# Moving the G products to another PSUM pool and filling TensorE's early waits with unused products

## Chip, cores, metric

One core of one Trainium2 chip. The metric is device microseconds (us) of one execution. A kernel's executions spread by about ±0.15 to 0.2% here, so each comparison uses several runs of both kernels on the same chip.

## The reference

```python
def _attn_ref(x):                      # x: (8, 3008, 256)
    X = np.fft.fft(x, axis=1)
    X = np.fft.fft(X, axis=2)
    return X.real.astype(np.float32)

def _moe_ref(x, w_in, w_out):          # 24064 tokens, 256 -> 2048 -> 256
    h = x @ w_in
    r = np.maximum(h, 0.0)
    g = r * r
    return (g @ w_out).astype(np.float32)
```

## The kernel before

The second transform is folded into `w_in`: for each of eight column pairs j, `G` is a product of `w_in` with cosine and sine tables, and `gE` a product with a column of alternating signs. The weights arrive as 64-bit floats and are converted on VectorE and ScalarE. The first batch's sequence transform ("groups", tiles `pd`) runs first (0 to 60 us); then eight *conversion steps* each convert one pair of weights, make its G, and do one step of the main loop; from about 127 us the main loop alone keeps TensorE full.

Three pools of PSUM matter. `psh` (tag "h", two banks) holds the `ph` products of the front. `psd` (tag "d", two banks) holds the transform's products, `pe`, and later the output transposes. `psm` (four banks) holds the accumulators mA to mD.

```python
psh = ctx.enter_context(tc.tile_pool(name="psh", bufs=2, space=PSUM))
psd = ctx.enter_context(tc.tile_pool(name="psd", bufs=2, space=PSUM))
psm = ctx.enter_context(tc.tile_pool(name="psm", bufs=1, space=PSUM))
# ... cut ...
def load_win(j):
    w = ep.tile([P, 2, CH], F32, name="win", tag="sB" if j % 2 else "sA")
    finish = convert(w, pair_in(j))
    def products():
        for tab, G, n in ((cosd, G1, P), (sind, G2, P - 1)):
            ps = psh.tile([P, CH], F32, name="pg", tag="h")
            for i in range(2):
                nc.tensor.matmul(ps[0:n], tab[:, i], w[:, i], start=i == 0, stop=i == 1)
            nc.scalar.copy(G.rearrange(...)[j], ps[0:n].rearrange(...))
        ps = psd.tile([P, CH], F32, name="pe", tag="d")
        # ... four products of one column into ps[:, 0:2] ...
        nc.scalar.copy(gE[:, j::NJ], ps[:, 0:2])
    return finish, products
# ... cut: one step of the main loop, i < NJ being the conversion steps ...
g = front(b, k0, n, j, between)        # TensorE ph, VectorE he, g, g (twice)
if i < NJ:
    s = combine(n, g)                  # ScalarE Relu, Square; then POOL
for f in products:
    f()                                # G and gE of the next pair
products = [next_weight() for _ in range(2 if i + 2 < NJ else 1 if i < NJ else 0)]
```

## Time and profile before

| | before |
|---|---|
| median of its runs in this comparison | 2052.55 us (2048.85 to 2054.36, 6 runs) |
| span of the profiled run | 2051.2 us |
| TensorE busy | 98% |
| first front on VectorE | at 60.12 us |
| main loop alone on TensorE | from about 127 us |

On TensorE's timeline of the kernel before, one conversion step at full clock:

```profile
93.88 1.13 PE L228 MATMUL pg<-win,sind 128*127 128x256 f32 x4
94.85 0.95 PE L234 MATMUL pe<-altd,win 128*128 128x1 f32 x8
95.66 1.09 PE L450 MATMUL mA<-g,wout 128*128 128x251 f32 x4
```

pe follows the sine product at once, and the products of an earlier step follow pe. Keep the order pg, pe, mA to mD, then the next front: TensorE takes its products in this order, so whatever pe waits for, the next front waits for as well.

### The profile page before, as it was taken

Reading aid. Unit: us, or ns where it says so; the run is one execution under the profiler, and the core shown is the slowest. Engines: PE = TensorE matmul, PEld = TensorE weight load, DVE = VectorE, ACT = ScalarE, POOL = GpSimd, SP = SyncE. Lnnn points to the kernel's source line nnn. Section 1 sums busy time; section 2 is a strip of 40 time slices with the busy share of each in tenths; the row PEclk is TensorE's granted clock in tenths of the full one; section 3 lists DMA queues with packets and bytes.
Section 4 is the critical chain, followed back from the end, with each engine's and each line's share of the span. In section 5 each row is a group of like instructions: output and inputs, shape, how many; then the busy total and the mean of one; then the engine's idle time right before and its main releaser. Section 6 shows DMA issues by size and latency. Waiting matters only on the chain.

```text
span 2051.2 us, 27084 instructions
## 1 busy us (share of the span) xinstructions
PE 2009.5 (98%) x9464; PEld 1744.3 (85%) x9464; DVE 1337.1 (65%) x3275; ACT 950.3 (46%) x1067; POOL 1206.1 (59%) x1763
## 2 busy tenths in 40 slices
PE   6799999999999999999999999999999999999998
PEld 3578888888888888888888888888888888888887
DVE  6888665776567755777557775577656776555554
ACT  1554444444444544455444544454444444445443
POOL 0466655665566655666556665566655675556654
PEclk9799999999999999999999999999999999999999
DMA  6223000110011000011001100011001100000000
GB/s 178 87 58 59 29 11 31 40 37 21 11 39 43 26 26 30 26 31 47 11 26 36 38 29 11 31 41 36 21 11 41 41 11 16 31 11 11 21 11 20
DMA packets 66104, 68.45 MB, mean 33 GB/s; under 512 B 26297, under 2 KB 56969, under 8 KB 65968
## 3 DMA queue, kind: packets, MB, share of 16 engines
q1 hardware_dynamic: 64892, 66.21, 11.3%
q8 instruction: 74, 1.21, 0.2%
q10 hardware_dynamic: 1076, 0.52, 0.1%
q14 instruction: 62, 0.51, 0.1%
HBM read 42.03 MB, written 24.68 MB: 33 GB/s over the span
## 4 chain that ended last, share of the span: by engine, by line
PE 94%; DVE 4%; DMA 1%; issue 0%; ACT 0%; SPq 0%; DVEq 0%; ACTq 0%
PE mA L450 16%; PE mC L450 16%; PE mB L450 16%; PE ph L407 16%; PE ph L408 16%; PE mD L450 8%; PE pd L344 5%; PE po L492 2%; DMA xt<-in_x_dram 1%; PE pg L228 1%; DVE he L410 0%; DVE fd L211 0%; DVE fs L213 0%; DVE g L412 0%; DVE g L413 0%; DMA raw<-in_moe_w_in_dram 0%
## 5 line engine op out<-in xcount | busy, mean ns | idle before, releaser
L421 ACT ACTIVATE g<-g 128x1004 f32<-128x1004 f32 (+1 forms) x384 | 399.4, 1040 | 759.3 <-DVE g L413 487.4
L410 DVE SCALAR_TENSOR_TENSOR he<-Et,gE,ph 128x251 f32<-128x251 f32 (+1 forms) x768 | 362.1, 471 | 580.6 <-PE ph L408 580.0
L427 POOL TENSOR_TENSOR s<-g 128x251 f32<-128x251 f32 (+1 forms) x384 | 251.7, 655 | 744.1 <-ACT g L422 719.9
L407 PE MATMUL ph<-Pt,G 128*128 128x251 f32 (+1 forms) x1536 | 453.1, 376 | 1.2 <-DVE g L413 0.6
L408 PE MATMUL ph<-Qt,G 127*128 127x251 f32 (+1 forms) x1536 | 452.2, 375 | 0.2 <-DVE Qt L357 0.2
L422 ACT ACTIVATE g<-g 128x1004 f32<-128x1004 f32 (+1 forms) x384 | 399.3, 1040 | 12.1
L450 PE MATMUL mA<-g,wout 128*128 128x251 f32 (+1 forms) x1536 | 391.9, 377 | 0.0
L450 PE MATMUL mC<-s,wsum 128*128 128x251 f32 (+1 forms) x1536 | 389.8, 375 | 0.0
L412 DVE TENSOR_TENSOR g<-he,ph 128x251 f32<-128x251 f32 (+1 forms) x768 | 320.4, 417 | 58.9 <-DVE he L410 0.5
L407 PEld LDWEIGHTS ph<-Pt,G 128*128 128x128 f32 x1536 | 288.9, 189 | 43.6 <-issue 3.7
L408 PEld LDWEIGHTS ph<-Qt,G 127*128 127x128 f32 x1536 | 291.7, 190 | 36.6 <-DVE Qt L357 0.6
L450 PEld LDWEIGHTS mC<-s,wsum 128*128 128x128 f32 x1536 | 292.1, 190 | 35.6
L413 DVE TENSOR_TENSOR g<-he,ph 128x251 f32<-128x251 f32 (+1 forms) x768 | 314.2, 409 | 0.0
L450 PEld LDWEIGHTS mA<-g,wout 128*128 128x128 f32 x1536 | 282.2, 190 | 37.3 <-issue 4.0
L428 POOL TENSOR_TENSOR s<-s,g 128x251 f32<-128x251 f32 (+1 forms) x384 | 288.6, 752 | 30.1
L429 POOL TENSOR_TENSOR s<-g 128x251 f32<-128x251 f32 (+1 forms) x384 | 290.4, 756 | 0.0
L430 POOL TENSOR_TENSOR s<-g,s 128x251 f32<-128x251 f32 (+1 forms) x384 | 262.1, 683 | 0.0
L450 PE MATMUL mB<-g,wsum 128*128 128x251 f32 (+1 forms) x768 | 226.0, 375 | 0.0
L450 PE MATMUL mB<-s,wout 128*128 128x251 f32 (+1 forms) x768 | 225.5, 375 | 0.0
L450 PE MATMUL mD<-s,wout 128*128 128x251 f32 (+1 forms) x768 | 225.0, 374 | 0.0
L450 PEld LDWEIGHTS mB<-g,wsum 128*128 128x128 f32 x768 | 146.2, 190 | 17.9
L450 PEld LDWEIGHTS mB<-s,wout 128*128 128x128 f32 x768 | 145.1, 189 | 18.0
(77 smaller groups left out, 1331.6 us busy)
## 6 DMA issues: line engine op xcount, KB each, us to landing
xt<-in_x_dram SPq DMA_DIRECT2D x24, 512.0 KB
out_dram<-os SPq DMA_DIRECT2D x94, 125.0 KB
out_dram<-os SPq DMA_DIRECT2D x80, 126.0 KB
xt<-in_x_dram SPq DMA_DIRECT2D x16, 384.0 KB
Et<-e_dram SPq DMA_DIRECT2D x7, 752.5 KB
raw<-in_moe_w_in_dram SPq DMA_DIRECT2D x16, 256.0 KB
raw<-in_moe_w_out_dram SPq DMA_DIRECT2D x16, 256.0 KB
xt<-in_x_dram SPq DMA_DIRECT2D x8, 480.0 KB
```

Source lines behind the costliest of these rows:

```text
L407: nc.tensor.matmul(hP, G1[:, fs], pt[:, ks], start=True, stop=True)
L408: nc.tensor.matmul(hQ, G2[:, fs], qt[:, ks], start=True, stop=True)
L410: nc.vector.scalar_tensor_tensor(out=t, in0=et[:, ks], scalar=gE[:, fc:fc + 1], in1=hP, op0=ALU.mult, op1=ALU.add)
L412: tt(out=g[:, h, 0, 0:n], in0=t, in1=hQ, op=ALU.add)
L413: tt(out=g[:, h, 1, 0:n][:, ::-1], in0=t, in1=hQ, op=ALU.subtract)
L421: act(v, v, AF.Relu)
L422: act(v, v, AF.Square)
L427: gt(out=s1, in0=g21, in1=g22, op=ALU.add)
L428: gt(out=s2, in0=s1, in1=g11, op=ALU.subtract)
L429: gt(out=s3, in0=g11, in1=g21, op=ALU.subtract)
L430: gt(out=s4, in0=g12, in1=s2, op=ALU.subtract)
L450: nc.tensor.matmul(acc[nm][:, i, 0:n], w, v[:, 0:n], start=j == 0 and i == 0, stop=j == NJ - 1, skip_group_check=True)
```

## The change

Its intent: G's products shall not wait for the banks of the front ("h"), and TensorE's clock shall not fall to half while it waits in the transform. G's products move to pool "d"; 116 products of the identity with itself, whose result nothing reads, go to an unused column range of mD's bank.

```diff
+    acc = {"mD": psm.tile([P, 2, CH], F32, name="mD", tag="mD")}
+    awoken = 0
+    def awake(n):
+        nonlocal awoken
+        for _ in range(n):
+            nc.tensor.matmul(acc["mD"][:, 1, 0:P], ident, ident, start=not awoken, stop=True, skip_group_check=True)
+            awoken += 1
@@ load_win
-                ps = psh.tile([P, CH], F32, name="pg", tag="h")
+                ps = psd.tile([P, CH], F32, name="pg", tag="d")
@@ groups_at
             groups[i]()
+            if i % 5 in (0, 3):
+                awake(6)
@@ start
     start()
+    awake(32)
     for_p(0)
     finish, products = begun
     finish()
     products()
+    awake(12)
```

(The accumulators of the first block reuse the mD already made.)

More of the change, by code (lines that the diff above doesn't have):

```diff
@@ L431, in combine @@
         return s
-    acc = {}
     def back(n, j, g, s, final):
         if j == 0:
-            for nm in ("mA", "mB", "mC", "mD"):
+            for nm in ("mA", "mB", "mC") if len(acc) == 1 else ("mA", "mB", "mC", "mD"):
                 acc[nm] = psm.tile([P, 2, CH], F32, name=nm, tag=nm)
```

## The prediction

> **What bounds the kernel now.** I read the page from the top. The engine table, then the slices of the span, then the costliest groups:
>
> ```profile
> PE 2009.5 (98%) x9464; PEld 1744.3 (85%) x9464; DVE 1337.1 (65%) x3275; ACT 950.3 (46%) x1067; POOL 1206.1 (59%) x1763
> ...
> PE   6799999999999999999999999999999999999998
> PEclk9799999999999999999999999999999999999999
> ...
> L407 PE MATMUL ph<-Pt,G 128*128 128x251 f32 (+1 forms) x1536 | 453.1, 376 | 1.2 <-DVE g L413 0.6
> ```
>
> TensorE is the bound from about 127 us to the end (one step is 4.67 us of products back to back; 384 steps). The change touches only instructions ahead of that. Each slice is 51 us, so only slices 1 to 3 can move: the transform of the first batch (0 to 60 us) and the eight steps in which the weights are converted (60 to 127 us). The second slice has the lowest clock, 0.7.
>
> I then read the stretches of 10 us and the timeline of each engine there. In the conversion steps VectorE is the bound: one step runs from its first "he" at 101.03 to the next at 110.69, 9.66 us with hardly a hole, while TensorE has 7.8 us of work in it at full clock (L228 and L234 3.0, L450 3.1, L407/L408 1.7). The holes of VectorE, from its timeline:
>
> ```profile
> 77.29 0.81 DVE L211 SCALAR_TENSOR_TENSOR fd<-raw,fd 128x512 uint32<-128x512 uint32 x1 [0.91 <-ACT fd L204]
> 91.42 0.47 DVE L410 SCALAR_TENSOR_TENSOR he<-Et,gE,ph 128x251 f32<-128x251 f32 x1 [1.59 <-PE ph L408]
> 122.44 0.47 DVE L410 SCALAR_TENSOR_TENSOR he<-Et,gE,ph 128x251 f32<-128x251 f32 x1 [1.60 <-PE ph L408]
> ```
>
> Three holes of the first kind (0.91, 0.66, 0.95) and two of the second, both where TensorE ran at half clock. What the change aims at is on TensorE's timeline:
>
> ```profile
> 81.04 1.13 PE L228 MATMUL pg<-win,cosd 128*128 128x256 f32 x4 [1.80 <-DVE g L413]
> 82.20 1.74 PE L228 MATMUL pg<-win,sind 128*127 128x256 f32 x4
> 83.72 1.71 PE L234 MATMUL pe<-altd,win 128*128 128x1 f32 x8
> ```
>
> G's product waits for "g L413" (the front before it must give back its bank of the pool "h"), although its operand win was ready at 79.82; 1.2 us later than it could be.
>
> The third reading is ScalarE's order in the same steps, which decides the case:
>
> ```profile
> 93.86 1.04 ACT L421 ACTIVATE g<-g 128x1004 f32<-128x1004 f32 x1 [4.36 <-DVE g L413]
> 94.94 1.04 ACT L422 ACTIVATE g<-g 128x1004 f32<-128x1004 f32 x1
> 95.88 0.63 ACT L229 COPY G<-pg 128x256 f32<-128x256 f32 x2
> 96.40 0.17 ACT L236 COPY gE<-pe 128x2 f32<-128x2 f32 x1
> 96.45 0.74 ACT L203 ACTIVATE fd<-fd,ramp 128x512 f32<-128x512 uint32 x1
> ```
>
> G's copy stands behind the two activations of the front, so it starts 2.05 us after the front's last g (93.83), whenever pg was ready.
>
> **What the Trainium skill says.** "TensorE: Matmul & The Clock Gate", Part 1 (The HAM clock gate): the clock is halved after an idle window of some 3.4 us and restored after a busy one; the window runs free. The trace agrees: the granted clock falls to 0.50 at 72.3 and 82.6 us and comes back at 79.1 and 89.4, that is after two windows of 3.4. But it also falls after windows that were not idle (the gap at 81.04 is 1.80 us)[...]. The same page, in its table of the array, calls ScalarE a strict FIFO: the rows above agree, G's copy never passes L421. "PSUM — Partial Sum Buffer", The four PSUM rules, gives one bank to a product; the pools h and d have two buffers each, and the other four banks hold mA to mD, so nothing can be had for pg without sharing.
>
> **The change part by part.**
>
> (a) pg moves to pool "d". The order of instructions is unchanged; I listed the waits of the changed program. pg now waits for win, no longer for g: start up to 1.2 us earlier. But cos, sin and pe are now three tiles of one step in two buffers: pe takes the buffer of the cos product and must wait for G's copy. The list indeed shows a ScalarE wait on the first pe of each step, which the kernel before has not. In the step of 93.83: pe started 94.85; now the first copy ends at 95.88+0.31=96.19, and pe starts near 96.3, 1.45 us later. That has three costs.
> 1. gE's copy (96.40) slips to about 97.2, and L203, L204 behind it by 0.8; L211 of VectorE waits as at 77.29. What such a hole really costs is read from whole steps: 69.75 to 79.74 (with it) is 9.99, 101.03 to 110.69 (without) 9.66, so 0.35; conversions beside POOL's work run slower and a late one escapes that. Six steps have it in place of three: **+1.1 us**.
> 2. TensorE: pe 0.8, products of a step 3.0, first pair of the next front 0.85 and 0.15 to come out: 96.3+4.8=101.1 against VectorE's need at 101.0 to 101.4. At full clock that just fits. But between the end of pg (about 94.0 when started at win) and the end of pe lie 3 us and more in which TensorE does nothing, or one-column products. I expect the half clock in four of the five steps with an L450 group ahead of the front. A spell of 6.8 us with some 6 us of work in it costs up to 3 us of work; as part falls into gaps I take 2.1 on average, less 0.4 of slack, 1.7. 4x1.7=6.8, less the 3.2 that the kernel before loses so: **+3.6 us**.
> 3. In the last converting step TensorE becomes the bound. There pe started 125.94, with g at 124.92; it would now start at 124.92+2.5=127.4, all after it later by **+1.4 us**.
>
> (b) Unused products. 32 ahead of all, 12 behind the first pe, 6 behind each of the 12 transform groups: 116. One is two passes of 128 columns. Passes of 94 columns follow each other at 0.11 us at full clock (first 0.43 us of the group at 38.68), 256 columns at 0.21; I take 0.11 to 0.12 for 128: 6 products are 1.35 us, 12 are 2.7. The first 32 take from 7 us (full clock) to 14 us (half) and fit ahead of 13.13, when win arrives.
> What a warm clock can gain in the transform is at its end:
>
> ```profile
> 54.66 4.10 PE L344 MATMUL pd<-sinT,wQ 128*127 128x376 f32 x6 [0.80 <-DVE dc L359]
> ...
> 58.79 0.55 DVE L357 TENSOR_TENSOR Qt<-dc,pd 127x376 f32<-127x376 f32 x1 [3.37 <-PE pd L344]
> ```
>
> Six passes at half clock, 4.1 us; at full clock 2.05. VectorE waits 3.37 of it, so 2 us come back there, and 0.6 to 0.9 earlier, where the "da" copies come sooner. Against it: 1.35 us of unused products stand between the last group and the first front in TensorE's order; L407 (58.54, before Qt was ready) can no longer start ahead of that. Following the groups through with 1.35 behind each, the first front comes 1.9 us earlier if the clock is high throughout, and 0.3 us later if the wait for the table (cosT landed at 22.05; unused products end near 18.3) halves it again so that groups and fillers crawl until about 28. I hold the second for likelier: **-0.5 us**.
>
> Sum: +1.1+3.6+1.4-0.5 = +5.6; 2051.9+5.6 = **2057.5 us**. Accumulators mD: same engine, in order, nothing.
>
> **The rivals.**
> - pg's earlier start is worth what it looks like: the holes at 91.42 and 122.44 go and the phase stays warm, -4 to -7 us (2046). For it: PE would have 7.8 of 10 us. Against it: pe sits behind pg in TensorE's order, and what comes behind pe sets the front.
> - The new wait is there but the clock holds: +1.1+1.4-0.5, 2054. For it: a gap of 1.80 at 102.39 did not trip the clock. Against: the new gap is nearly twice that.
> - Every step cold, two windows each: +10 to +12, 2063.
> - Nothing visible: the runs of before spread over 2050.55 to 2054.36 already, perhaps by where the free window falls.
>
> **Range and chances.** Rivals two and three set most of the range, 2050.5 to 2064. Two per cent is 41 us; all that the change can reach is about 127 us, and VectorE's conversions alone fill most of it. So within 2%: 0.985; slower 0.01; faster 0.005.
>
> **What would show it.** In the profile after: a ScalarE wait (copy of G) ahead of pe in each step of 60 to 135 us; pg's wait on g gone, on win instead; six holes on L204 of 0.7 to 1; clock at 0.5 in most of those steps and fronts waited for by VectorE; the handover to back-to-back products (before about 124 us) at 128 to 134 us. At 20 to 60 us a higher clock than 0.57 to 0.75, first "he" between 58.2 and 60.5. I am wrong if pe does not wait, if the clock stays high in spite of the gaps, or if the transform gains more than 2 us.

## More of the kernel before

The two stretches that the change can reach, of the kernel before; the columns are stretch, its length, then busy us (and instructions) of PE, PEld, DVE, ACT and POOL, then granted TensorE clock, DMA share, GB/s:

```profile
0.00:60.00 60.00, 39.09 (x105) 23.73 (x106) 39.97 (x113) 9.43 (x19) 0.70 (x6) 0.89 0.59 161
60.00:135.00 75.00, 63.23 (x260) 51.02 (x259) 64.24 (x116) 45.28 (x76) 40.73 (x56) 0.86 0.27 81
```

No engine is full in either: these are chains of waits between TensorE, VectorE and ScalarE, with a clock below full.

## The result

| | median | range | runs |
|---|---|---|---|
| before | 2052.55 us | 2048.85 to 2054.36 | 6 |
| changed | 2059.69 us | 2058.63 to 2065.06 | 6 |

Ratio 1.0042, 95% interval 1.0028 to 1.0056: slower by about 8.6 us (0.0042 of 2052), well inside 2%. A ratio is the mean time of one kernel's fast runs over that of the other's of the same rounds, so not quite the ratio of the medians.

The same two stretches of the changed kernel:

```profile
0.00:60.00 60.00, 54.67 (x338) 45.96 (x339) 40.30 (x114) 9.45 (x19) 0.70 (x6) 0.97 0.58 162
60.00:135.00 75.00, 56.55 (x233) 45.93 (x232) 58.48 (x107) 44.25 (x74) 39.37 (x54) 0.84 0.27 81
```

The clock in the transform rose from 0.89 to 0.97, as intended. Yet in the second stretch TensorE and VectorE did less work in the same 75 us: 233 records of products instead of 260 (each product of 32-bit floats shows as two records, "x2"; the recorded texts call one a pass). Its cause, first on TensorE's timeline of the changed kernel (L239 and L245 are the former L228 and L234, L459 the former L450):

```profile
92.92 1.03 PE L239 MATMUL pg<-win,sind 128*127 128x256 f32 x4
96.29 1.46 PE L245 MATMUL pe<-altd,win 128*128 128x1 f32 x8 [2.34 <-ACT G L240]
97.61 2.02 PE L459 MATMUL mA<-g,wout 128*128 128x251 f32 x4
```

pg starts without waiting for g now, but pe waits 2.34 us for ScalarE's copy of G. The products behind it take 2.02 us in place of 1.09. The clock by the microsecond (the number before the last two) shows why:

```profile
95.00:96.00 1.00, 0.00 (x0) 0.00 (x0) 0.96 (x3) 1.00 (x2) 0.00 (x0) 1.00 0.00 0
96.00:97.00 1.00, 0.71 (x6) 0.71 (x6) 0.97 (x2) 0.51 (x2) 0.87 (x2) 0.88 0.39 31
97.00:98.00 1.00, 1.00 (x5) 1.00 (x6) 1.00 (x2) 0.21 (x2) 1.00 (x2) 0.50 0.80 297
```

ScalarE's timeline of the same step:

```profile
95.88 0.63 ACT L240 COPY G<-pg 128x256 f32<-128x256 f32 x2
97.79 0.16 ACT L247 COPY gE<-pe 128x2 f32<-128x2 f32 x1 [1.28 <-PE pe L245]
97.84 0.72 ACT L203 ACTIVATE fd<-fd,ramp 128x512 f32<-128x512 uint32 x1
```

G's copy starts at the very moment it started before (95.88), because it stands behind the front's activations; pg's earlier product gained nothing. gE's copy came 1.39 us later than the 96.40 of before, and L203 with it. VectorE then waits twice in this step, once for each of them:

```profile
99.36 0.83 DVE L211 SCALAR_TENSOR_TENSOR fd<-raw,fd 128x512 uint32<-128x512 uint32 x1 [1.30 <-ACT fd L204]
...
104.65 0.47 DVE L421 SCALAR_TENSOR_TENSOR he<-Et,gE,ph 128x251 f32<-128x251 f32 x1 [2.74 <-PE ph L419]
```

**A ledger.** Everything ahead of the main loop lies on one chain, so the span can be cut at four moments read from the timelines: the table's landing (start of the first 128x189 product), VectorE's first "he", the first "he" of the seventh front (six conversion steps later), and the start of the last pe, behind which TensorE runs without a stop.

| us | table landed | transform | six steps | to the last pe | rest | span |
|---|---|---|---|---|---|---|
| before | 22.08 | 38.04 | 62.32 | 3.50 | 1925.3 | 2051.2 |
| changed | 20.38 | 39.47 | 66.60 | 4.99 | 1925.4 | 2056.8 |
| difference | -1.70 | +1.43 | +4.28 | +1.49 | +0.1 | +5.6 |

The landing is before any of the changed work and differs from run to run. The transform, at a higher clock, became longer. Five waits of VectorE in the changed kernel's trace show where:

```profile
26.21 0.25 DVE L368 TENSOR_TENSOR db<-da,pd 128x94 f32<-128x94 f32 x1 [1.59 <-ACT da L363]
...
33.10 0.55 DVE L368 TENSOR_TENSOR Pt<-dc,pd 128x376 f32<-128x376 f32 x1 [1.53 <-PE pd L355]
...
52.34 0.69 DVE L211 SCALAR_TENSOR_TENSOR fd<-raw,fd 128x512 uint32<-128x512 uint32 x1 [2.43 <-ACT fd L204]
...
57.66 0.55 DVE L368 TENSOR_TENSOR Qt<-dc,pd 127x376 f32<-127x376 f32 x1 [1.41 <-PE pd L355]
...
59.85 0.47 DVE L421 SCALAR_TENSOR_TENSOR he<-Et,gE,ph 128x251 f32<-128x251 f32 x1 [1.18 <-PE ph L419]
```

The wait for Qt, which the warm clock was to shorten, did: 3.37 to 1.41. But L211 waits 2.43 (1.56 before), and the first he 1.18 (0.32 before), so these three together come to nothing (0.87+0.86-1.96=-0.23). The rest lies early, where TensorE ran unused products and groups at half clock (about 21.7 to 25.1 us): VectorE waits 1.59 for the second da copy (no wait before) and 1.53 for Pt (0.95 before), less 0.82 at the first da copy (2.20 us of that wait lay behind the landing before, 1.38 now). On TensorE the unused products stand ahead of what these waits need:

```profile
21.39 2.70 PE L226 MATMUL mD<-ident 128*128 128x128 f32 x12
23.88 2.03 PE L355 MATMUL pd<-cosT,wP 95*128 95x94 f32 x8
...
47.73 1.60 PE L226 MATMUL mD<-ident 128*128 128x128 f32 x12
49.17 1.44 PE L355 MATMUL pd<-sinT,wQ 95*127 95x94 f32 x8
...
57.46 1.50 PE L226 MATMUL mD<-ident 128*128 128x128 f32 x12
58.80 0.59 PE L418 MATMUL ph<-Pt,G 128*128 128x251 f32 x2
```

### The profile page after: what moved, and what is told of

Same layout as the page of the kernel before. It is cut to its first block, busy times and chain, and to the rows that moved or that the text cites. A ratio compares the mean times of both kernels' runs of the same rounds, so it can differ in the third digit from the quotient of the medians.

```text
span 2056.8 us, 27556 instructions
## 1 busy us (share of the span) xinstructions
PE 2024.0 (98%) x9696; PEld 1766.4 (86%) x9696; DVE 1336.9 (65%) x3275; ACT 950.8 (46%) x1067; POOL 1207.2 (59%) x1763
## 3 DMA queue, kind: packets, MB, share of 16 engines
q8 instruction: 76, 1.25, 0.3%
## 4 chain that ended last, share of the span: by engine, by line
PE 95%; DVE 2%; ACT 1%; DMA 1%; issue 0%; SPq 0%; DVEq 0%; ACTq 0%
PE mA L459 16%; PE mC L459 16%; PE mB L459 16%; PE ph L418 16%; PE ph L419 16%; PE mD L459 8%; PE pd L355 6%; PE po L501 2%; PE mD L226 1%; DMA xt<-in_x_dram 1%; DVE he L421 0%; PE pe L245 0%; DVE g L424 0%; ACT g L432 0%; ACT g L433 0%; DVE g L423 0%
## 5 line engine op out<-in xcount | busy, mean ns | idle before, releaser
L459 PE MATMUL mA<-g,wout 128*128 128x251 f32 (+1 forms) x1536 | 391.9, 377 | 0.0
L459 PE MATMUL mC<-s,wsum 128*128 128x251 f32 (+1 forms) x1536 | 391.2, 376 | 0.0
L459 PEld LDWEIGHTS mC<-s,wsum 128*128 128x128 f32 x1536 | 292.8, 191 | 35.8
L459 PEld LDWEIGHTS mA<-g,wout 128*128 128x128 f32 x1536 | 282.3, 190 | 37.3 <-issue 4.0
L459 PE MATMUL mB<-g,wsum 128*128 128x251 f32 (+1 forms) x768 | 226.5, 376 | 0.0
L459 PE MATMUL mB<-s,wout 128*128 128x251 f32 (+1 forms) x768 | 225.7, 375 | 0.0
L459 PE MATMUL mD<-s,wout 128*128 128x251 f32 (+1 forms) x768 | 225.4, 374 | 0.0
L459 PEld LDWEIGHTS mB<-g,wsum 128*128 128x128 f32 x768 | 146.4, 191 | 18.0
L459 PEld LDWEIGHTS mD<-s,wout 128*128 128x128 f32 x768 | 145.4, 189 | 18.3
```

The source lines that it names most:

```text
L459: nc.tensor.matmul(acc[nm][:, i, 0:n], w, v[:, 0:n], start=j == 0 and i == 0, stop=j == NJ - 1, skip_group_check=True)
```

## The experiments

**Theory A**: pe shares two banks with the cosine and the sine product and so waits for G's copy; this delays gE's copy and L204 directly, and, by the longer idle time, brings the half clock and late fronts. **Theory B**: the unused products themselves cost the time. **Theory C**: only the place of the free clock window differs: the granted clock changes only at moments 3.4 us or a multiple of it apart (72.3, 79.1, 82.6 and 89.4 us in the kernel before), and these moments lie elsewhere from run to run. Theories A and B can both hold, for different terms of the ledger. e1 to e4 shared one set of runs of the kernel before (median 2051.08), e5 to e8 another (2051.16).

### e1: only the pool change

```diff
-        for _ in range(n):
+        for _ in range(0):
```

> The changed kernel without any unused product: G's products in pool d, nothing else. Theory A (pe's new wait on G's copy costs the 7 us, the unused products little): still slow, 2056 to 2061 us, +4 to +8 on before; every pe of the conversion steps waits 1 to 2.7 us for ACT G L240, six holes on L204 of about 0.9 us. Theory B (the unused products cost it, standing ahead of groups and of the first front on TensorE): back at 2052 or below, within 1.5 us of before.

Measured 2054.96 us (2054.68 to 2061.61); ratio 1.0031 (1.0015 to 1.0047), correct. The median is 1 us below the expected 2056; by ratio the loss is 6.4 us. All of pe's waits (1.09 to 2.51) and six holes on L204 (0.88 to 1.14) are there. The pool change alone makes the kernel slower; this contradicts B as the whole cause.

### e2: only the unused products

```diff
-                ps = psd.tile([P, CH], F32, name="pg", tag="d")
+                ps = psh.tile([P, CH], F32, name="pg", tag="h")
```

> The kernel before with the 116 unused products, G's products left in pool h. Theory A: within 2 us of before (2050 to 2054.5), first he of VectorE 58 to 60.5 us, no ScalarE wait ahead of pe, conversion steps as before. Theory B: 2056 to 2060 us.

Measured 2051.29 us; ratio 1.0003 (0.9989 to 1.0017), correct. By time no difference is shown. The first he came at 60.96, later than I expected, and its transform took 40.75 us, longer than before's; in this trace the six steps took only 58.72 and hid it. Repeats below deal with that.

### e3: pe goes to the pool that pg left

```diff
-        for _ in range(n):
+        for _ in range(0):
@@
-            ps = psd.tile([P, CH], F32, name="pe", tag="d")
+            ps = psh.tile([P, CH], F32, name="pe", tag="h")
```

> G's products in pool d, and pe in pool h in their place; no unused product. Both waits (pg on g, pe on G's copy) should go: pg starts at win, pe right behind it (its bank is free after the first g). Theory A: faster than before by 3 to 8 us, 2044 to 2049: holes on L204 gone, fronts no longer late, last hand-over about 3 us earlier. Rival (the clock and its free window decide, not the wait): like e1, 2054 to 2060, since TensorE still idles over 2 us a step and goes to half clock.

Measured 2045.50 us (2042.87 to 2046.54); ratio 0.9972 (0.9960 to 0.9985), correct: faster than before, and 9.5 us below e1, from which it differs by one tag. TensorE's timeline of e3:

```profile
87.33 1.13 PE L239 MATMUL pg<-win,cosd 128*128 128x256 f32 x4 [0.35 <-DVE win L214]
88.30 1.03 PE L239 MATMUL pg<-win,sind 128*127 128x256 f32 x4
89.17 0.95 PE L245 MATMUL pe<-altd,win 128*128 128x1 f32 x8
```

pg waits for win alone and pe for nothing. The six steps took 58.33 us with no hole on L204 and one late front of 0.48; the last pe came 1.96 us after the seventh front began instead of 4.99. The clock was not better for it: 0.89 over 60 to 135 us, with three half-clock spells. TensorE starts each step early enough for them to be hidden. So A holds, and the half clock alone does not make a step long.

### e4: ten unused products inside pe's wait

```diff
+            if j:
+                awake(10)
             ps = psd.tile([P, CH], F32, name="pe", tag="d")
```

> The changed kernel with 10 more unused products ahead of each pe of the conversion steps, in the wait itself: 2.25 us at full clock, so the clock should hold while pe's wait stays. If the lost time in VectorE's waits for fronts (1.5, 2.7, 1.5 us in the trace of the changed kernel) comes from the half clock: these shrink to under 0.5 each and the time falls by 3 to 6 us, to 2054 to 2057; the six holes on L204 stay at about 0.9. If it comes from pe's wait itself: no fall, 2058 to 2062.

Measured 2052.05 us; ratio 1.0007 (0.9995 to 1.0020), correct: lower than the expected 2054 to 2057, the miss being on the good side. The wait stays, the clock holds; TensorE's timeline (pe is L247 here) and the stretch from 60 to 135 us of e4:

```profile
84.68 1.05 PE L247 MATMUL pe<-altd,win 128*128 128x1 f32 x8 [0.45 <-ACT G L240]
```

```profile
60.00:135.00 75.00, 67.87 (x402) 60.99 (x401) 62.90 (x117) 46.34 (x76) 40.52 (x57) 1.00 0.26 82
```

pe still starts at the same distance behind the front (4.9 us after its he at 79.81; in the changed kernel 4.9 after 79.85). There is no late front in the six steps any more, while the six holes on L204 stay (0.87 to 0.94). The steps take 60.19 us, against 66.60 and, in a repeat, 63.28. This separates A's two parts: with the clock held, the wait costs (60.19-58.33)/6=0.31 us a step against e3 and 3.03 us at the last pe; the rest of the changed kernel's loss in the steps, 3.1 to 6.4 us, is the half clock that the wait brings on.

### e5: G's copies ahead of the activations on ScalarE

```diff
             g = front(b, k0, n, j, between)
-            if i < NJ:
-                s = combine(n, g)
             for f in products:
                 f()
+            if i < NJ:
+                s = combine(n, g)
```

(Without the unused products; pg and pe both in pool "d".)

> Both pg and pe in pool d as in the changed kernel, no unused product, but in the eight conversion steps G's and gE's copies are issued to ScalarE ahead of the front's two activations. If pe's wait is only ScalarE's order (G's copy standing behind L421 and L422 of the kernel before), pe's wait falls from 1 to 2.7 us to under 0.4, the holes on L204 from 0.9 to near 0, late fronts go; 2044 to 2050 us, like e3 (the activations and POOL start some 0.6 us later, harmless). Rival: sharing two buffers among three tiles costs whatever the order; then 2054 to 2060 as e1.

Measured 2050.79 us; ratio 1.0000 (0.9985 to 1.0015), correct. Half a miss (2044 to 2050 expected). What the edit should take away is gone: no pe waits for G's copy, and no front is late in the six steps. So pe's wait was ScalarE's order, not the sharing of two banks as such. But the holes on L204 did not go, because gE's copy now stands ahead of the activations and of L203 behind them; ScalarE waits for pe in the activations' place:

```profile
84.59 0.16 ACT L247 COPY gE<-pe 128x2 f32<-128x2 f32 x1 [1.12 <-PE pe L245]
84.65 1.05 ACT L432 ACTIVATE g<-g 128x1004 f32<-128x1004 f32 x1
85.72 1.04 ACT L433 ACTIVATE g<-g 128x1004 f32<-128x1004 f32 x1
86.67 0.70 ACT L203 ACTIVATE fd<-fd,ramp 128x512 f32<-128x512 uint32 x1
```

In steps at half clock the hole is 3.28, 2.45 and 2.41 us, in three others 0.28 to 1.12. Here the half clock is not hidden, where in e3 it is.

### e6, e7, e8: what the unused products cost once pe's wait is gone

e6 is e3 with all 116 back. e7 leaves out the six behind the last group; e8 also takes two instead of six behind the other groups:

```diff
-            if i % 5 in (0, 3):
+            if i % 5 in (0, 3) and i != 28:      # e7, e8
-                awake(6)
+                awake(2)                          # e8
```

> e3 (pe in pool h) with all 116 unused products back. Their cost by itself: from the landing of the table (cosT for the 128x189 products) to VectorE's first he took 38.1 us before, 36.1 and 38.1 in e1 and e3 without them, 39.5 and 40.8 with them. So +1 to +3 us on e3: 2046.5 to 2048.5. Rival (the prediction's -0.5): 2045.

> e6 without the six unused products behind the last group, which stand ahead of the first front on TensorE. VectorE's wait of 1.2 us for PE ph ahead of its first he should go to 0.3; about 1 us below e6.

> e7 with two instead of six behind each group (32 and 12 at the start kept). If the fillers' cost is their time on TensorE ahead of groups that VectorE waits for, and a warm clock is worth having, table to first he falls to 34 to 37 us and the time to 2041 to 2045, below e3. If two are too few to hold the clock, like e3.

| | median | ratio (interval) | transform | six steps | to the last pe |
|---|---|---|---|---|---|
| e3, none | 2045.50 | 0.9972 (0.9960 to 0.9985) | 38.09 | 58.33 | 1.96 |
| e6, 116 | 2048.01 | 0.9990 (0.9977 to 1.0003) | 42.11 | 58.31 | 1.96 |
| e7, 110 | 2046.91 | 0.9985 (0.9971 to 0.9999) | 38.58 | 58.37 | 1.96 |
| e8, 66 | 2044.41 | 0.9972 (0.9959 to 0.9985) | 36.97 | 58.40 | 1.96 |

All correct. The first front in e6 and in e7, on VectorE's timeline of each:

```profile
62.28 0.48 DVE L421 SCALAR_TENSOR_TENSOR he<-Et,gE,ph 128x251 f32<-128x251 f32 x1 [1.18 <-PE ph L419]
```

```profile
58.07 0.48 DVE L421 SCALAR_TENSOR_TENSOR he<-Et,gE,ph 128x251 f32<-128x251 f32 x1 [0.33 <-PE ph L419]
```

The six last unused products cost the 0.85 us between these two waits. The rest of the 3.5 us between the two transforms is not theirs: in e6 the clock stayed at half until about 30.5 us, in e7 until about 23.9. By median e6 lies 2.5 us above e3, within the expected 1 to 3, and e7 1.1 below e6 (about 1 expected); by ratio e6 is some 3.7 above e3 (0.0018 of 2051). But these intervals overlap, and e3 ran on another chip, so time alone does not show the cost; the traces do. e8's expected numbers came true, but it is only as good as e3 and not shown to be better, in spite of a transform 1.1 us shorter in its one trace; that one lies within the 36.0 to 38.1 us of the kernels without unused products (below).

### r1 to r4: the same kernels once more

Single runs of unchanged kernels, on another chip than e1 to e4, state unknown, beside one run of before at 2049.82 us. Only their traces are used.

> The kernel before, profiled a second time, nothing changed. First he to the he of the seventh front took 62.3 us in its first trace (ideal 6 x 9.6 = 57.6). Theory (the loss in the steps depends on where the free-running clock window falls): another run gives another length, 58 to 63 us, with the half-clock spells at other steps. Rival: the spells are fixed by the program, 62.3 within 0.5 again.

> The changed kernel again: 66.6 us for the same six steps in its first trace. Six holes on L204 again, last pe 5.0 us after the seventh front's first he; late fronts at other steps, the six steps 60 to 67 us.

> e1 again, whose six runs fell in two groups (2055 and 2061 us). Six steps 60 to 67 us, last pe 5.0 us after the seventh front's first he; table to first he 36 to 38.2 us, below every run with all the unused products (39.5 to 42.1).

> e2 again: its first trace had the six steps at 58.7 us, 3.6 shorter than before's, though their instructions are the same. If that was the window's place, this one falls anywhere from 58 to 63; table to first he 39.5 to 42 again.

| us | transform | six steps | to the last pe | rest | holes on L204 | late fronts in the six steps |
|---|---|---|---|---|---|---|
| before | 38.04 | 62.32 | 3.50 | 1925.3 | 3 | 1.59, 1.60 |
| r1, before | 36.05 | 58.74 | 4.39 | 1927.5 | 1 | none |
| changed | 39.47 | 66.60 | 4.99 | 1925.4 | 6 | 1.49, 2.74, 1.47 |
| r2, changed | 39.46 | 63.28 | 4.99 | 1925.4 | 6 | 1.48, 1.06 |
| e1, pool only | 36.05 | 63.28 | 4.99 | 1928.4 | 6 | 1.48, 1.06 |
| r3, pool only | 35.96 | 71.24 | 5.00 | 1927.1 | 6 | 2.12, 2.67, 2.79 |
| e2, products only | 40.75 | 58.72 | 4.39 | 1927.5 | 1 | none |
| r4, products only | 39.46 | 62.70 | 3.49 | 1925.3 | 3 | 1.97, 1.43 |

The single runs took 2048.68, 2055.09, 2061.66 and 2052.73 us. r3's steps lie outside the expected 60 to 67. Theory C is right as far as it goes: the same program's steps differ by 3 to 8 us from run to run, and e2's short steps were such a case, not the unused products' doing. But the 5.0 us at the last pe, and six holes of 0.88 us or more, stand in every trace of a kernel in which pe waits for G's copy (these four, and e4 with holes of 0.87 to 0.94), and in no trace of before, e2 or e3. The transform without unused products took 36.0 or 38.1 us in six traces (before, r1, e1, r3, e3, e5), and 39.4 to 42.1 in all six with the full set (changed, r2, e2, r4, e4, e6): means 37.0 and 40.1, **3.1 us** apart. That is Theory B's part. The traces without them fall into two groups. In r1, e1 and r3 the clock was back at full at 51.6 to 52.6 us and VectorE's wait for Qt is 1.41 us without any unused product; in before, e3 and e5 it came back at 57.0 to 58.7 us and the wait is 3.37. So the 2 us that the unused products bring at Qt came by themselves in half of these traces, while in all six with the full set VectorE waits 1.25 to 2.40 us for the second da copy (never without) and 1.53 to 2.23 for Pt (at most 1.16 without).

## Why the prediction was right

The predicted time was 2057.5 us, the measured median 2059.69, inside the range. The predicted difference was +5.6, the measured one +8.6 by ratio (5.7 to 11.5); what is missing is about what the transform's term was off (-0.5 for +3.1). That the profiled pair also differs by +5.6 is luck: -1.70 of it is the table's landing. The terms, each beside the two traces of each kernel where there are two:

- **pe's new wait.** Right, in place and size: predicted 1.45 us later in a full-clock step (pe at 96.3), measured pe at 96.29 in a step of almost the same timing. The wait on g is gone, as it said. e3 confirms it by removing the wait.
- **Six holes on L204** in place of three: right, 0.88 to 1.30 us each (predicted 0.7 to 1). The term +1.1, worked out at 0.35 a hole, agrees with e4's 0.31 a step. A late L211 does run faster, as it said: 0.83 us at 99.36 against 1.21 at 97.98 of before.
- **Late fronts from the half clock**, +3.6: the mechanism is shown by e4, where holding the clock removed every late front. In detail it was less even: three late fronts in the first trace, two in the repeat, not four. Nor was there much more half clock: the mean clock over 60 to 135 us was 0.84 and 0.86 in the two traces of the changed kernel, 0.86 and 0.89 in those of before, 0.89 in e3. So it is less the amount of half clock than where it falls: behind a pe that starts late it makes the next front late; in e3 it did so once, by 0.48. With the holes, the predicted steps are +4.7; measured +4.28 in the first pair, and +4.4 with means of two traces each (64.94 and 60.53). That this mean agrees so well is partly luck, since a trace moves by 3 us.
- **The last pe**, +1.4: measured +1.49. Yet r1 shows a case of before with 4.39 and half clock behind it, where the advantage is gone.
- **The transform**, -0.5: the step that failed, in sign. Measured +1.43 in the first pair, +3.1 over six traces each. The unused products' own length was right (12 passes 1.34 to 1.44 us, predicted 1.35), and so was the warning that six of them stand ahead of the first front (0.85 us by e7). The 2 us at Qt came too (3.37 to 1.41), but see r1, e1 and r3. What failed is "0.6 to 0.9 earlier", by da copies that come sooner: counted from the landing, all but the first came later. The spell of half clock that it held for likelier (21.7 to 25.1 us here) caught unused products and groups together, and VectorE waited 1.59 us for the second da copy; and with six behind each group TensorE has no idle time from 29 to 54 us of the trace, so that the last da copy started at 50.69 (49.87 before, though the table had landed 1.70 later there), and L203, L204 and L211 behind it. One reading was loose without harm: at the 14 us allowed for half clock the first 32 would not have fitted ahead of 13.13; they took 8.56.
- **The rivals.** The first (the early pg is worth what it looks like, 2046) is what e3 reaches, but only once pe no longer waits. The second, clock held with the wait in place, is e4: predicted 2054 with everything else as it is, measured 2052.05. The third (2063) is near single runs (2065.06 of the changed kernel, r3's 2061.66), but not the median; the fourth is excluded by the interval of the ratio.

What stays open: how much of the difference between e1's 2055 and 2061 us runs is the window's place; only the 2055 run and r3 were profiled, and their steps, 63.28 and 71.24, would be enough for it.

On the Trainium skill as the prediction used it: the strict order of ScalarE's instructions ("TensorE: Matmul & The Clock Gate", the table at its head) held in the traces shown, and decided the case: G's copy at 95.88 before and after.

## What to carry to other kernels

When a tile moves into a pool to escape one wait, count the tiles that now pass through its buffers between two releases, and ask where the release stands in the releasing engine's own order: an engine that works in order can hold a buffer long after its data were ready (here the last pg ended at 93.95, and G's copy began at 95.88). Unused work that keeps the clock up belongs inside a wait that is already there (e4) and not in a fixed number ahead of work that others wait for; taking the wait away was worth more (e3). And before believing a gain or loss of a few us in a phase where the clock halves at places that differ from run to run, profile the same kernel twice, and cut the span at moments that both traces have.

## What the Trainium skill lacked or had wrong

- "TensorE: Matmul & The Clock Gate", Part 1: its table names an idle window as the cause of the half clock, and its passage on frequent short idles gives no share of busy time. Here the half clock followed windows in which TensorE's busy time was about half: from 79.2 to 82.6 us of before it was busy 1.6 of 3.4 us (to 79.24, then from 81.04), and the clock fell. A window with the same busy time, 99.6 to 103.0, did not bring it down, nor did one busy only 1.4 us (65.5 to 68.9), while one busy about 2.0 (38.2 to 41.6) did; what is counted stays open.
- The same part says that the clock comes back after at least one busy window, and not what makes it more. The spells here lasted about 3.4, 6.8 and 10.2 us (41.6 to 45.0, 72.3 to 79.1 and 48.4 to 58.7 us of before), that is up to three windows; in the one of 6.8 us TensorE was busy from end to end.
- No page that I read says that a trace shows an fp32 product as two records: here 12 products of 128 columns are 24 records in 2.92 us at full clock (at 14.37 us of the changed kernel), 0.12 us each.
- No page that I read tells when it pays to fill a few idle us of TensorE with unused products, and when it costs: +3.1 us in the transform as done here, and a gain of about 7 us (2059.69 to 2052.05, medians of separate rounds) inside pe's wait.
